# The second layer in blocks of 512 tokens instead of 256, with 512 moving columns in its first product

## The chip, the cores and the metric

One NeuronCore of a Trainium2 chip runs the whole program. The metric is the device time of one execution in microseconds. Names of engines: PE is TensorE, PEld its weight loads, DVE VectorE, ACT ScalarE, POOL GpSimd, SP the engine that issues the DMAs.

## What is computed

```python
attn = attention(q, k, v, phi)        # 8 x 8 x 576 x 64, with a memory of 32
x = attn as (4608 tokens, 512)
h = x @ moe_w_in                      # 512 -> 2048
x = (h - tanh(h)) @ moe_w_out         # 2048 -> 512: first layer
h = x @ moe2_w_in
g = where(h > 0, h, exp(min(h, 0)) - 1)
out = g @ moe2_w_out                  # second layer
```

All inputs are float32. A product is made of three matmuls: each operand is split into a high part (rounded) and the remainder, a = 0 and a = 1 in the code, and high·high, high·low and low·high are added up in PSUM.

## The kernel before, in words

Attention and the first layer come first (`Attention`, `Moe1`), in blocks of 288 tokens and four sweeps over the hidden units. The first layer's output is left in DRAM as four partial sums, `x2_dram`, which the second layer adds up. The second layer (`Moe2`) goes over 18 blocks of `TB` = 256 tokens and in each over 8 slices `pg` of 256 hidden units: 144 steps, called one by one from `step2`. All instructions stand in program order on their engines; nothing is rearranged by a scheduler.

One step of `step2` issues, in this order:

- `h_unit`, the first product: two halves `j` of 128 hidden units, for each 12 matmuls (4 pieces of the contraction, three part products) with the weights as the stationary operand and 256 tokens of `x` as moving columns. Both halves lie in one PSUM tile of 128 x 512.
- `e_a`, `e_b`, `e_c`, the elementwise part of min, tanh, exp and max on DVE and ACT; `e_c`, one step later, splits the result into high (ACT, L469) and low (POOL, L470).
- `prep`, a piece of the next block's input: `load_x` (one of the four partial sums into the pool `xr`, three buffers), `add_x` (DVE, L426), and `split_x` (high on ACT, L432, low on POOL, L433).
- `o_unit`, the second product of two steps earlier (`LAG2`): for each of two groups `tg` of 128 tokens six matmuls with the elementwise result as the stationary operand and 512 output columns. In the last slice of a block each group is copied from PSUM into a tile `o` (L486 on ACT, L488 on DVE; the pool `o` has two buffers) and stored.

The accumulators of `o_unit` are two tags of the PSUM pool `ps_o` with two buffers each; `ps_m` has three banks for the first product, `ps_c` one.

```python
        def step2(idx):
            if idx < len(seq):
                n, pg = seq[idx]
                m2.h_unit(n, pg)
                m2.e_a(n, pg)
            if 1 <= idx <= len(seq):
                m2.e_c(*seq[idx - 1])
            if idx < len(seq):
                m2.e_b(n, pg)
                prep(n + 1, pg)
            if idx >= LAG2:
                m2.o_unit(*seq[idx - LAG2])
```

The hand-over: in the last four blocks of the first layer (`bi` 60 to 63) a queue `soon` prepares the second layer's first block. One entry is taken in each half `i` of such a block before the first `x_unit`, and from `bi` 61 on a second one ahead of the second. That second place stands, on DVE, before the copy of `x` (L397) and the first layer's elementwise instructions of `g_c` (L367 to L369). Steps 0 and 1 of the second layer are issued among the last eight `x_unit`s of the first.

Of the kernel before, what the change touches and what calls it, by code (L numbers as in the profile page):

```python
# [24 lines left out]
NPG = DFF // 256  # L25
NSW = 4
TB = 256
# [379 lines left out]
class Moe2:  # L407


    def __init__(self, tc, x2_dram, out):  # L410
        self.tc, self.nc, self.x2_dram, self.out = tc, tc.nc, x2_dram, out
        self.x, self.h, self.e, self.acc = {}, {}, {}, {}
        self.w = {}

    def load_x(self, n, sw):
        t = self.xr_p.tile([128, 4, TB], F32, tag="xr", name="xr")
        self.nc.sync.dma_start(out=t, in_=self.x2_dram[sw, :, :, n * TB:(n + 1) * TB])
        if sw == 0:
            self.x[n] = [t]
        else:  # L420
            self.x[n].append(t)

    def add_x(self, n):
        raw = self.x[n]
        t = raw.pop(1)
        self.nc.vector.tensor_tensor(raw[0], raw[0], t, op=ALU.add)  # L426

    def split_x(self, n):
        nc = self.nc
        raw = self.x[n][0]  # L430
        x = self.x_p.tile([128, 2, 4, TB], F32R, tag="x", name="x")
        nc.scalar.activation(x[:, 0], raw, ACTF.Copy)  # L432
        nc.gpsimd.tensor_tensor(x[:, 1], raw, r32(x[:, 0]), op=ALU.subtract)  # L433
        self.x[n] = x

    def h_unit(self, n, pg):
# [10 lines left out]
        self.h[n, pg] = [ps]  # L447

    def e_a(self, n, pg):
        nc, w = self.nc, self.h[n, pg]  # L450
        hm = self.ew.tile([128, 2, TB], F32, tag="hm", name="hm")
        t = self.ps_t.tile([128, 2, TB], F32, tag="c", name="t_ps")
# [5 lines left out]
    def e_b(self, n, pg):  # L458
        nc = self.nc
        ps, hm, t = self.h[n, pg]  # L460
# [4 lines left out]
    def e_c(self, n, pg):  # L465
        nc = self.nc
        hm = self.h.pop((n, pg))[1]
        e = self.e_p.tile([128, 2, 2, TB], F32R, tag="e", name="e")
        nc.scalar.activation(e[:, 0], hm, ACTF.Copy)  # L469
        nc.gpsimd.tensor_tensor(e[:, 1], hm, r32(e[:, 0]), op=ALU.subtract)  # L470
        self.e[n, pg] = e

    def o_unit(self, n, pg):
        nc = self.nc
        if pg == 0:
            self.acc[n] = [self.ps_o.tile([128, DM], F32, tag=f"o{i}", name="o_ps") for i in range(2)]
        e, w4 = self.e.pop((n, pg)), self.w["o", pg]
        for tg in range(2):
            for j in range(2):
                for i, (a, b) in enumerate(((0, 0), (0, 1), (1, 0))):  # L480
                    nc.tensor.matmul(self.acc[n][tg], lhsT=e[:, a, j, 128 * tg:128 * tg + 128], rhs=w4[:, b, j, :],  # L481
                                     start=(pg == 0 and j == 0 and i == 0), stop=(pg == NPG - 1 and j == 1 and i == 2))
            if pg == NPG - 1:
                o = self.o_p.tile([128, DM], F32, tag="o", name="o")
                if tg == 0:
# [17 lines left out]
def moe_kernel(tc, q, k, v, phi, w1, w2, w3, w4, out):  # L503
    nc = tc.nc
    with ExitStack() as top, tc.manual_schedule():
# [156 lines left out]
        def open_l2():  # L662
# [6 lines left out]
            m2.x_p = pool("xs", 2)  # L669
# [11 lines left out]
        seq = [(n, pg) for n in range(NB2) for pg in range(NPG)]  # L681
        LAG2 = 2

        def prep(n, step):

            if n < NB2:
                if step in (3, 4, 5):
                    m2.add_x(n)
                if step < NSW:
                    m2.load_x(n, step)  # L690
                if step == 6:
                    m2.split_x(n)

        def step2(idx):
            if idx < len(seq):
                n, pg = seq[idx]
                m2.h_unit(n, pg)
                m2.e_a(n, pg)
            if 1 <= idx <= len(seq):
                m2.e_c(*seq[idx - 1])  # L700
            if idx < len(seq):
                m2.e_b(n, pg)
                prep(n + 1, pg)
# [4 lines left out]
        for bi, (ss, bp, sub, j) in enumerate(blocks):  # L708
            sw, n = 2 * ss + sub, 4 * bp + j
            if bi == 60:  # L710
# [3 lines left out]
                soon = deque([steps(0), steps(1), steps(2), steps(3), weight("i", 0), steps(4, 5), weight("i", 1),  # L714
                              steps(6), weight("o", 0), weight("i", 2), weight("o", 1)])
# [90 lines left out]
        first = deque([("o", 2, w_first), ("i", 3, w_next), ("o", 3, w_next)])  # L806
# [7 lines left out]
        for ctx in (ps_h_ctx, l1c, l1a):  # L814
            ctx.close()
        m2.ps_o = new(l2, "ps_o", 2, space=PSUM)
# [3 lines left out]
                      if (kind, k) not in (("o", 4), ("i", NPG)))  # L820
# [35 lines left out]
```

## Time and profile before

| | |
|---|---|
| median of 3 runs | 1751.77 us (1746.34 to 1754.0) |
| span of the profiled execution | 1749.5 us |
| PE busy, share of the span | 1637.8 us, 94% |
| PEld | 1513.9 us, 87% |
| DVE | 1222.6 us, 70% |
| ACT | 954.2 us, 55% |
| POOL | 760.9 us, 43% |
| DMA | 238.42 MB, mean 136 GB/s |
| mean granted clock of PE | 0.970 |

The span runs from the first to the last instruction of the profiled execution; the device time of a run holds what lies around it too, and the median stands 2.3 us above this span. Matmuls are pipelined and the trace models their ends, so a PE that is busy may still be standing before each matmul; how fast it goes is read from the starts of consecutive units in the chain of waits, not from its busy share.

### The profile page before, as it was taken

The page shows a single profiled execution, that of the slowest core. Times are in us where ns is not written, and L with a number is a line of the kernel's source. Part 1 is how long each engine was busy: PE and PEld are TensorE (multiplying, and loading weights), DVE is VectorE, ACT ScalarE, POOL GpSimd, SP SyncE. Part 2 cuts the span into 40 slices and gives each one's busy share as a digit, 9 for nine tenths or more (in the row PEclk, how much of TensorE's full clock was granted, in tenths as well). Part 3 has the DMA queues.
Part 4 walks back from the last instruction along what each step waited for, and adds up shares of the span by engine and source line. Part 5 has one row for each costly group of instructions (what it writes and reads, how often), then busy time and mean ns, then how long its engine had stood idle before and what let it go on. Part 6 is the DMA issues. An engine that isn't in the chain of part 4 may idle for free.

```text
span 1749.5 us, 30362 instructions
## 1 busy us (share of the span) xinstructions
PE 1637.8 (94%) x11632; PEld 1513.9 (87%) x11632; DVE 1222.6 (70%) x1821; ACT 954.2 (55%) x1713; POOL 760.9 (43%) x537
## 2 busy tenths in 40 slices
PE   5668989988998999999989999999999999999998
PEld 3557878887898999999989999999999999999997
DVE  5769666778899999998965555555555555555554
ACT  2456666677878888888863333333333333333332
POOL 2245545546666667676752222222222222222222
PEclk7669999999999999999999999999999999999999
DMA  8765555467566456666578312211212212111110
GB/s 213 198 177 148 179 158 181 147 199 232 187 211 200 167 182 208 215 223 208 203 230 316 130 60 61 61 54 56 61 61 61 61 61 61 58 52 58 58 31 25
DMA packets 140936, 238.42 MB, mean 136 GB/s; under 512 B 8184, under 2 KB 102392, under 8 KB 138744
## 3 DMA queue, kind: packets, MB, share of 16 engines
q1 hardware_dynamic: 140792, 236.49, 43.3%
q8 instruction: 92, 1.51, 0.4%
q14 instruction: 52, 0.43, 0.1%
HBM read 159.78 MB, written 75.50 MB: 134 GB/s over the span
## 4 chain that ended last, share of the span: by engine, by line
PE 75%; DVE 10%; ACT 5%; DMA 5%; issue 3%; POOL 2%; ACTq 0%; DVEq 0%; POOLq 0%; SPq 0%
PE h_ps L444 23%; PE o_ps L481 23%; PE x_ps L388 15%; PE h_ps L343 8%; PE vw_ps L328 3%; DVE s L368 2%; DMA w_dram<-wst 2%; DVE vw L333 1%; DMA raw<-in_moe_w_in_dram 1%; DMA phi<-in_phi_dram 1%; DVE h_ps L367 1%; DVE s L369 1%; PE km L156 1%; ACT t L354 1%; ACT big L357 1%
## 5 line engine op out<-in xcount | busy, mean ns | idle before, releaser
L388 PE MATMUL x_ps<-g,w 128*128 128x288 f32 x3072 | 442.8, 298 | 13.7 <-ACT x L395 6.7
L470 POOL TENSOR_TENSOR e<-hm,e 128x512 fp32r<-128x512 f32 x144 | 186.5, 1295 | 587.0 <-ACT e L469 442.6
L444 PEld LDWEIGHTS h_ps<-x,wi 128*128 128x128 f32 x3456 | 429.8, 190 | 11.7
L388 PEld LDWEIGHTS x_ps<-g,w 128*128 128x128 f32 x3072 | 421.5, 190 | 18.6 <-ACT x L395 8.0
L444 PE MATMUL h_ps<-x,wi 128*128 128x256 f32 x3456 | 433.2, 282 | 0.0
L481 PE MATMUL o_ps<-wo,e 128*128 128x512 f32 x1728 | 423.8, 394 | 0.7 <-POOL e L470 0.7
L481 PEld LDWEIGHTS o_ps<-wo,e 128*128 128x128 f32 x1728 | 314.9, 188 | 64.9 <-POOL e L470 1.1
L455 ACT ACTIVATE t_ps<-hm 128x512 f32<-128x512 f32 x144 | 86.7, 602 | 514.3 <-DVE hm L454 514.3
L362 POOL TENSOR_TENSOR v<-t,u 128x576 f32<-128x576 f32 x128 | 183.9, 1437 | 197.6 <-ACT u L355 163.9
L343 PE MATMUL h_ps<-p,vw 128*128 128x288 f32 x1536 | 235.8, 304 | 7.9 <-DVE s L369 6.3
L376 POOL TENSOR_TENSOR g<-s,g 128x576 fp32r<-128x576 f32 x128 | 199.0, 1555 | 96.1 <-ACT g L375 91.1
L461 DVE SCALAR_TENSOR_TENSOR hm<-hm,t_ps 128x512 f32<-128x512 f32 x144 | 99.1, 688 | 200.6 <-ACT hm L456 200.6
L343 PEld LDWEIGHTS h_ps<-p,vw 128*128 128x128 f32 x1536 | 217.0, 194 | 12.9 <-issue 7.9
L454 DVE TENSOR_SCALAR hm<-h_ps 128x512 f32<-128x512 f32 x144 | 99.6, 692 | 138.5 <-PE h_ps L444 138.5
L368 DVE SCALAR_TENSOR_TENSOR s<-s,v 128x576 f32<-128x576 f32 x128 | 139.9, 1093 | 3.7 <-POOL v L362 2.6
L354 ACT ACTIVATE t<-h_ps 128x576 f32<-128x576 f32 x128 | 83.2, 650 | 72.7 <-PE h_ps L343 28.4
L369 DVE COPY_PREDICATED s<-big,h_ps 128x576 f32<-128x576 uint32 x128 | 106.6, 833 | 12.0 <-ACT u L355 0.5
L333 DVE TENSOR_TENSOR vw<-vw_ps,vw 64x512 fp32r<-64x512 f32 x128 | 87.8, 686 | 36.5 <-ACT vw L331 34.5
L356 ACT ACTIVATE s<-u,bias 128x576 f32<-128x576 f32 x128 | 99.5, 778 | 24.0 <-POOL g L376 14.6
L328 PE MATMUL vw_ps<-w,vm 128*128 128x256 f32 x480 | 78.9, 304 | 28.2 <-ACT x L395 14.7
L463 DVE TENSOR_TENSOR hm<-hm,h_ps 128x512 f32<-128x512 f32 x144 | 99.0, 687 | 5.0
L462 DVE SCALAR_TENSOR_TENSOR hm<-hm,t_ps 128x512 f32<-128x512 f32 x144 | 98.9, 687 | 4.9
(85 smaller groups left out, 1827.5 us busy)
## 6 DMA issues: line engine op xcount, KB each, us to landing
x_dram<-x SPq DMA_DIRECT2D x128, 288.0 KB
xr<-x_dram SPq DMA_DIRECT2D x72, 512.0 KB
p<-p_dram SPq DMA_DIRECT2D x62, 576.0 KB
raw<-in_moe_w_in_dram SPq DMA_DIRECT2D x32, 512.0 KB
raw<-in_moe_w_out_dram SPq DMA_DIRECT2D x32, 512.0 KB
w_dram<-wst SPq DMA_DIRECT2D x32, 512.0 KB
kv<-in_k_dram SPq DMA_DIRECT2D x16, 576.0 KB
kv<-in_v_dram SPq DMA_DIRECT2D x16, 576.0 KB
```

The costliest lines, as they stand in the source:

```text
L328: nc.tensor.matmul(ps[:, kc], lhsT=vm[:, a, p, :], rhs=wi[:, b, p, :], start=(i == 0), stop=(i == 2))
L333: nc.vector.tensor_tensor(lo, src, r32(hi), op=ALU.subtract)
L343: nc.tensor.matmul(ps[:, j, :NB], lhsT=vw[a][:, kc, 128 * j:128 * j + 128], rhs=p[:, kc, b, :], start=(k == 0), stop=(k == 5))
L354: nc.scalar.activation(t, w[0], ACTF.Tanh)
L362: nc.gpsimd.tensor_tensor(v, t, u, op=ALU.mult)
L368: nc.vector.scalar_tensor_tensor(s, s, G_B, v, op0=ALU.add, op1=ALU.mult)
L369: nc.vector.copy_predicated(s, big.bitcast(U32), d)
L376: nc.gpsimd.tensor_tensor(g[:, 1], s, r32(g[:, 0]), op=ALU.subtract)
L388: nc.tensor.matmul(ps, lhsT=wo[pg][:, a, j, 128 * dm:128 * dm + 128], rhs=g[:, b, j, :], start=(k == 0), stop=(k == 11))
L444: nc.tensor.matmul(ps[:, j], lhsT=w3[:, a, kc, 128 * j:128 * j + 128], rhs=x[:, b, kc, :], start=(k == 0), stop=(k == 11))
L470: nc.gpsimd.tensor_tensor(e[:, 1], hm, r32(e[:, 0]), op=ALU.subtract)
L481: nc.tensor.matmul(self.acc[n][tg], lhsT=e[:, a, j, 128 * tg:128 * tg + 128], rhs=w4[:, b, j, :], start=(pg == 0 and j == 0 and i == 0), s ...
```

## The change

Blocks of 512 tokens: 9 blocks, in each 16 slices `k` of 128 hidden units (`pg, j = divmod(k, 2)` picks the weights), 144 steps as before. `h_unit` has 12 matmuls with 512 moving columns. `o_unit` goes over four groups of 128 tokens with three matmuls each; the four accumulators have one buffer each, so as much PSUM as before. `x` is loaded, added and split in two halves of 256 tokens, four loads each. The first block's two halves are prepared in `soon`, which has 14 entries instead of 11, and some weights are loaded later.

```diff
-TB = 256
+TB = 512
+NU2 = DFF // 128
...
-    def load_x(self, n, sw):
-        t = self.xr_p.tile([128, 4, TB], F32, tag="xr", name="xr")
-        self.nc.sync.dma_start(out=t, in_=self.x2_dram[sw, :, :, n * TB:(n + 1) * TB])
...
+    def load_x(self, n, half, sw):
+        t = self.xr_p.tile([128, 4, TB // 2], F32, tag="xr", name="xr")
+        t0 = n * TB + half * (TB // 2)
+        self.nc.sync.dma_start(out=t, in_=self.x2_dram[sw, :, :, t0:t0 + TB // 2])
+        self.raw.append(t)
...
+    def split_x(self, n, half):
+        nc = self.nc
+        raw = self.raw.pop()
+        if half == 0:
+            self.x[n] = self.x_p[n % 2].tile([128, 2, 4, TB], F32R, tag="x", name="x")
+        hi, lo = (self.x[n][:, t, :, half * (TB // 2):(half + 1) * (TB // 2)] for t in range(2))
...
-        ps = self.ps_h.tile([128, 2, TB], F32, tag="m", name="h2_ps")
-        for j in range(2):
-            k = 0
-            for kc in range(4):
-                for a, b in ((0, 0), (0, 1), (1, 0)):
-                    nc.tensor.matmul(ps[:, j], lhsT=w3[:, a, kc, 128 * j:128 * j + 128], rhs=x[:, b, kc, :],
-                                     start=(k == 0), stop=(k == 11))
-                    k += 1
+        pg, j = divmod(k, 2)
...
+        ps = self.ps_h.tile([128, TB], F32, tag="m", name="h2_ps")
+        i = 0
+        for kc in range(4):
+            for a, b in ((0, 0), (0, 1), (1, 0)):
+                nc.tensor.matmul(ps, lhsT=w3[:, a, kc, 128 * j:128 * j + 128], rhs=x[:, b, kc, :],
+                                 start=(i == 0), stop=(i == 11))
+                i += 1
...
-            self.acc[n] = [self.ps_o.tile([128, DM], F32, tag=f"o{i}", name="o_ps") for i in range(2)]
+            self.acc[n] = [self.ps_o.tile([128, DM], F32, tag=f"o{i}", name="o_ps") for i in range(TB // 128)]
...
+        for tg in range(TB // 128):
+            for i, (a, b) in enumerate(((0, 0), (0, 1), (1, 0))):
+                nc.tensor.matmul(self.acc[n][tg], lhsT=e[:, a, 128 * tg:128 * tg + 128], rhs=w4[:, b, j, :],
+                                 start=(k == 0 and i == 0), stop=(k == NU2 - 1 and i == 2))
+            if k == NU2 - 1:
...
-                if tg == 0:
+                if tg % 2 == 0:
...
         def prep(n, step):
             if n < NB2:
+                half, step = divmod(step, NU2 // 2)
...
-                soon = deque([steps(0), steps(1), steps(2), steps(3), weight("i", 0), steps(4, 5), weight("i", 1),
-                              steps(6), weight("o", 0), weight("i", 2), weight("o", 1)])
+                soon = deque([steps(0), steps(1), steps(2), steps(3), weight("i", 0), steps(4, 5, 6), steps(8),
+                              steps(9), steps(10), weight("o", 0), steps(11), steps(12, 13, 14), weight("i", 1),
+                              weight("o", 1)])
...
-        first = deque([("o", 2, w_first), ("i", 3, w_next), ("o", 3, w_next)])
+        first = deque([("i", 2, w_first), ("o", 2, w_next), ("i", 3, w_next)])
...
-        m2.ps_o = new(l2, "ps_o", 2, space=PSUM)
+        m2.ps_o = new(l2, "ps_o", 1, space=PSUM)
+        m2.x_p.append(new(l2, "xs2", 1))
```

What this moves on the engines shows in three places of the program's order. Square brackets name the engine or DMA queue on which an instruction waits, as far as the program asks for it.

PE where one block's accumulators pass to the next; a row is one or several matmuls, `x9` nine of them. Before, a first product and the next block's first second product:

```order
L444 MATMUL h_ps<-x,wi_11283 128x256 [waits DVE_49,PE_49]
L444 MATMUL h_ps<-x,wi_11283 128x256 x23
L481 MATMUL o_ps<-wo_11264,e 128x512 [waits Activation_49]
L481 MATMUL o_ps<-wo_11264,e 128x512
L481 MATMUL o_ps<-wo_11264,e 128x512 [waits Pool_49]
L481 MATMUL o_ps<-wo_11264,e 128x512 x9
```

With the change, the same place:

```order
L443 MATMUL h_ps<-x,wi_11395 128x512 [waits DVE_49]
L443 MATMUL h_ps<-x,wi_11395 128x512 x11
L480 MATMUL o_ps<-wo_11285,e 128x512 [waits Activation_49]
L480 MATMUL o_ps<-wo_11285,e 128x512
L480 MATMUL o_ps<-wo_11285,e 128x512 [waits Pool_49]
L480 MATMUL o_ps<-wo_11285,e 128x512 [waits DVE_49]
L480 MATMUL o_ps<-wo_11285,e 128x512 x2
L480 MATMUL o_ps<-wo_11285,e 128x512 [waits Activation_49]
L480 MATMUL o_ps<-wo_11285,e 128x512 x2
L480 MATMUL o_ps<-wo_11285,e 128x512 [waits DVE_49]
L480 MATMUL o_ps<-wo_11285,e 128x512 x2
```

The first product has 12 matmuls of 512 columns instead of 24 of 256, and the next block's first second product waits at each of its four accumulators, in turn for ACT and DVE, where before it waited for its own operands alone.

DVE at the same place; `o<-o_ps` is the copy of an accumulator, the row behind it the next step's minimum (L454 before, L453 with the change). Before:

```order
L463 TENSOR_TENSOR hm<-hm,h_ps 128x512 [waits DVE_49]
L488 COPY o<-o_ps 128x512 [waits DMAHW3_49,DMAHW2_49,PE_49]
L454 TENSOR_SCALAR hm<-h_ps 128x512 [waits PE_49,Pool_49]
L461 SCALAR_TENSOR_TENSOR hm<-hm,t_ps 128x512 [waits Activation_49]
L462 SCALAR_TENSOR_TENSOR hm<-hm,t_ps 128x512 [waits DVE_49]
```

With the change:

```order
L462 TENSOR_TENSOR hm<-hm,h_ps 128x512 [waits DVE_49]
L487 COPY o<-o_ps 128x512 [waits DMAHW7_49,DMAHW6_49,PE_49]
L487 COPY o<-o_ps 128x512 [waits DMAHW2_49,DMAHW3_49,DVE_49,PE_49]
L453 TENSOR_SCALAR hm<-h_ps 128x512 [waits PE_49,Pool_49]
L460 SCALAR_TENSOR_TENSOR hm<-hm,t_ps 128x512 [waits Activation_49]
L461 SCALAR_TENSOR_TENSOR hm<-hm,t_ps 128x512 [waits DVE_49]
```

There are two copies ahead of the next minimum instead of one, and the second waits for DMAs that read the buffer of `o` (the third and fourth copies take the buffers of the first and second), beside PE.

DVE in the last blocks of the first layer, from the copy of `x` of one unit on. Before:

```order
L397 COPY x<-x_ps 128x288 [waits DMAHW0_49,PE_49]
L367 TENSOR_TENSOR h_ps<-h_ps,t 128x2x288 [waits Activation_49]
L368 SCALAR_TENSOR_TENSOR s<-s,v 128x576 [waits Activation_49,Pool_49]
L369 COPY_PREDICATED s<-big,h_ps 128x576 [waits DVE_49,Activation_49]
L397 COPY x<-x_ps 128x288 [waits DMAHW2_49,PE_49]
L367 TENSOR_TENSOR h_ps<-h_ps,t 128x2x288 [waits Activation_49]
L368 SCALAR_TENSOR_TENSOR s<-s,v 128x576 [waits Activation_49,Pool_49]
```

With the change (lines moved by one):

```order
L398 COPY x<-x_ps 128x288 [waits DMAHW0_49,PE_49]
L368 TENSOR_TENSOR h_ps<-h_ps,t 128x2x288 [waits Activation_49]
L369 SCALAR_TENSOR_TENSOR s<-s,v 128x576 [waits Activation_49,Pool_49]
L370 COPY_PREDICATED s<-big,h_ps 128x576 [waits DVE_49,Activation_49]
L424 TENSOR_TENSOR xr<-xr 128x1024 [waits DMAHW4_49,DMAHW3_49]
L424 TENSOR_TENSOR xr<-xr 128x1024 [waits DMAHW6_49,DVE_49]
L424 TENSOR_TENSOR xr<-xr 128x1024 [waits DMAHW1_49,DVE_49]
L398 COPY x<-x_ps 128x288 [waits DMAHW2_49,PE_49]
L368 TENSOR_TENSOR h_ps<-h_ps,t 128x2x288 [waits Activation_49]
L369 SCALAR_TENSOR_TENSOR s<-s,v 128x576 [waits Activation_49,Pool_49]
```

Three additions stand between the elementwise work of two units, each with a load to wait for; before, DVE has nothing there.

## Rows read from the trace of the kernel before

**Rows 1.** The page, 40 slices of the span, busy tenths and granted clock in tenths.
```profile
PE   5668989988998999999989999999999999999998
...
PEclk7669999999999999999999999999999999999999
```

**Rows 2.** Chain of waits from 1303 us (start us, us, engine, tile, line, instructions).
```profile
1308.00 2.75 PE o_ps L481 x12
1310.75 2.82 PE h_ps L444 x24
...
1324.74 2.81 PE o_ps L481 x12
...
1333.18 2.88 PE h_ps L444 x24
```

**Rows 3.** Timeline 1251 to 1266 us (start us, us, engine, line, operation, operands; idle before).
```profile
1254.30 0.58 ACT L486 ACTIVATE o<-o_ps 128x512 f32<-128x512 f32 x1
...
1255.95 0.69 DVE L488 COPY o<-o_ps 128x512 f32<-128x512 f32 x1
...
1257.21 2.91 PE L481 MATMUL o_ps<-wo,e 128*128 128x512 f32 x12
1257.49 0.69 DVE L454 TENSOR_SCALAR hm<-h_ps 128x512 f32<-128x512 f32 x1 [0.85 <-PE h_ps L444]
...
1260.19 1.30 POOL L470 TENSOR_TENSOR e<-hm,e 128x512 fp32r<-128x512 f32 x1 [4.38 <-PE o_ps L481]
```

**Rows 4.** Timeline 1300 to 1312 us.
```profile
1300.96 0.68 DVE L488 COPY o<-o_ps 128x512 f32<-128x512 f32 x1
...
1302.51 0.52 SPq L417 DMA_DIRECT2D xr<-x_dram  x1
```

**Rows 5.** DMA in slices of 0.25 us: GB/s 1254 to 1264, tenths 1299 to 1309.
```profile
GB/s 0 0 0 0 0 0 41 262 238 295 180 33 0 0 66 123 213 164 221 188 82 16 8 25 12 102 164 225 344 377 389 381 111 0 0 0 0 0 0 0
...
DMA  0000002727941098951285999982000000000000
```

**Rows 6.** Chain of waits at the end of the kernel.
```profile
1745.01 0.69 DVE o L488
```

**Rows 7.** Timeline 880 to 930 us.
```profile
899.55 4.83 DVE L426 TENSOR_TENSOR xr<-xr 128x1024 f32<-128x1024 f32 x2
...
899.76 3.22 PE L343 MATMUL h_ps<-p,vw 128*128 128x288 f32 x12 [5.93 <-DVE s L369]
...
909.04 1.05 ACT L432 ACTIVATE x<-xr 128x1024 fp32r<-128x1024 f32 x1
...
910.63 2.40 POOL L433 TENSOR_TENSOR x<-xr,x 128x1024 fp32r<-128x1024 f32 x1
...
914.45 1.98 DVE L368 SCALAR_TENSOR_TENSOR s<-s,v 128x576 f32<-128x576 f32 x1 [0.93 <-POOL v L362]
...
917.26 0.44 DVE L397 COPY x<-x_ps 128x288 f32<-128x288 f32 x1
...
922.36 3.03 PE L444 MATMUL h_ps<-x,wi 128*128 128x256 f32 x24
```

**Rows 8.** Chain of waits 878 to 931 us.
```profile
881.94 13.80 DMA xr<-x_dram
...
902.98 4.57 PE x_ps L388 x24
907.55 1.62 PE h_ps L343 x12
...
919.33 3.19 PE x_ps L388 x24
```

**Rows 9.** Line L426 from 880 to 1000 us (ns min/median/max).
```profile
L426 DVE TENSOR_TENSOR xr<-xr x7: 1217/1220/2432, 895.8 to 997.2; 128x1024 f32<-128x1024 f32 x7
```

**Rows 10.** Stretches: window, us, busy us of PE, PEld, DVE, ACT, POOL; clock, DMA, GB/s.
```profile
905.00:905.50 0.50, 0.50 (x4) 0.50 (x4) 0.50 (x2) 0.00 (x0) 0.00 (x0) 0.50 0.84 183
```

**Rows 11.** Stretch of first product, same columns.
```profile
1305.20:1307.70 2.50, 2.50 (x23) 2.50 (x22) 1.44 (x3) 0.00 (x0) 1.29 (x1) 1.00 0.23 82
```

More of the change, by code (lines that the diff above doesn't have):

```diff
@@ L428, in split_x @@
[L428 to L436 removed]
+        self.w, self.raw = {}, []
+    def load_x(self, n, half, sw):
[3 more added lines that the diff above has]
+        self.raw.append(t)
@@ L453, in e_a @@
+        self.h[n, k] = [ps]
+    def e_a(self, n, k):
+        nc, w = self.nc, self.h[n, k]
+        hm = self.ew.tile([128, TB], F32, tag="hm", name="hm")
+        t = self.ps_t.tile([128, TB], F32, tag="c", name="t_ps")
         w += [hm, t]
@@ L463, in e_b, with e_c, o_unit @@
         nc.vector.tensor_tensor(hm, hm, ps, op=ALU.max)
-    def e_c(self, n, pg):
+    def e_c(self, n, k):
         nc = self.nc
-        hm = self.h.pop((n, pg))[1]
-        e = self.e_p.tile([128, 2, 2, TB], F32R, tag="e", name="e")
+        hm = self.h.pop((n, k))[1]
+        e = self.e_p.tile([128, 2, TB], F32R, tag="e", name="e")
         nc.scalar.activation(e[:, 0], hm, ACTF.Copy)
         nc.gpsimd.tensor_tensor(e[:, 1], hm, r32(e[:, 0]), op=ALU.subtract)
-        self.e[n, pg] = e
-    def o_unit(self, n, pg):
+        self.e[n, k] = e
+    def o_unit(self, n, k):
         nc = self.nc
-        if pg == 0:
-            self.acc[n] = [self.ps_o.tile([128, DM], F32, tag=f"o{i}", name="o_ps") for i in range(2)]
[L477 to L483, printed above, removed]
+        pg, j = divmod(k, 2)
+        if k == 0:
+            self.acc[n] = [self.ps_o.tile([128, DM], F32, tag=f"o{i}", name="o_ps") for i in range(TB // 128)]
+        e, w4 = self.e.pop((n, k)), self.w["o", pg]
+        for tg in range(TB // 128):
[3 more added lines that the diff above has]
+            if k == NU2 - 1:
                 o = self.o_p.tile([128, DM], F32, tag="o", name="o")
-                if tg == 0:
+                if tg % 2 == 0:
                     nc.scalar.activation(o, self.acc[n][tg], ACTF.Copy)
@@ L668, in open_l2 @@
             m2.xr_p = pool("xr", 3)
-            m2.x_p = pool("xs", 2)
+            m2.x_p = [pool("xs", 1)]
             m2.ew = pool("ew", 2)
@@ L680, in moe_kernel @@
         NB2 = NT // TB
-        seq = [(n, pg) for n in range(NB2) for pg in range(NPG)]
+        seq = [(n, k) for n in range(NB2) for k in range(NU2)]
         LAG2 = 2
@@ L686, in prep @@
             if n < NB2:
+                half, step = divmod(step, NU2 // 2)
                 if step in (3, 4, 5):
-                    m2.add_x(n)
+                    m2.add_x()
                 if step < NSW:
-                    m2.load_x(n, step)
+                    m2.load_x(n, half, step)
                 if step == 6:
-                    m2.split_x(n)
+                    m2.split_x(n, half)
         def step2(idx):
             if idx < len(seq):
-                n, pg = seq[idx]
-                m2.h_unit(n, pg)
-                m2.e_a(n, pg)
+                n, k = seq[idx]
+                m2.h_unit(n, k)
+                m2.e_a(n, k)
             if 1 <= idx <= len(seq):
@@ L701, in step2 @@
             if idx < len(seq):
-                m2.e_b(n, pg)
-                prep(n + 1, pg)
+                m2.e_b(n, k)
+                prep(n + 1, k)
             if idx >= LAG2:
```

26 lines of the change are left out of this document (9 added, 17 removed).

## The prediction

> **What bounds the kernel now.** I read the page's forty slices first: from slice 22 on TensorE (PE) is at 9 tenths or more, its clock at full [rows 1]. That is the second layer, the only stage that the change touches apart from the hand-over into it, so I read its chain of waits next. Through the eight steps of a 256-token block the chain holds nothing but PE: a unit of the first product (24 matmuls, 2.82 to 2.88 us), then one of the second (12 matmuls, 2.75 to 2.81 us), eight times without a gap (16 such rows) [rows 2]. DVE, ACT and POOL wait for PE there. So in this layer time is won by shorter PE units and lost by anything that makes PE wait; there are 18 × 8 = 144 steps. The execution profiled spans 1749.5 us; the median of the three runs is 1751.8, 2.3 us more, which I carry along as it is.
>
> **The change, part by part.**
>
> *1. 24 matmuls of 256 columns become 12 of 512.* The steps stay 144 (9 blocks × 16 slices), with the same products. Nothing in this trace has a first product at 512 columns; the nearest rows are those of the second product, 12 matmuls of 512 columns each with a weight load of its own. The middle of the units is 2.85 us against 2.78 [rows 2], that is 118.8 ns for 256 columns and 231.7 for 512: most of a matmul's excess over its columns seems to go with the columns, little with the instruction. If a unit of the first product takes what one of the second does, a step gains 0.07 us: 144 × 0.07 = **−10.1 us**. Bounds from the same rows: slowest first against fastest second unit, 2.88 − 2.75 = 0.13, −18.7 us; fastest against slowest, 2.82 − 2.81 = 0.01, −1.4 us. A loss isn't excluded by a mechanism, but no unit of 512 columns took longer than one of 2 × 256. I take the middle.
>
> The Trainium skill ("TensorE: Matmul & The Clock Gate", section "Back-to-back issue gap") has columns ÷ 2.4 GHz plus about 2.5 ns for each warm matmul: 109.2 ns at 256 columns, 215.8 at 512. The rows are 9.6 and 15.9 ns above that, so they disagree. By the rule, 1728 matmuls fewer give an estimated −4.3 us, and the sum below would end at +6.5 instead of +0.7.
>
> *2. Four single accumulators.* Before, a block's two accumulators have two buffers each; now the next block's first second-product unit writes where the last one has just been read out. Four copies go through the pool `o`, which still has two buffers: the third and fourth copy wait until the stores of the first and second have landed. In the trace ACT copies accumulator 0 at 1254.30 and DVE accumulator 1 at 1255.95 to 1256.64; the next second-product unit starts at 1257.21 [rows 3]. With three matmuls for each accumulator it would reach the fourth after nine, 9 × 0.232 = 2.09 us, at 1259.30. The store of accumulator 1 has landed about 2.1 us after its copy in one place (copy's end 1301.64, data until about 1303.75) and 2.6 to 3.4 in another (data until 1259.25, a remnant of 8 to 25 GB/s to 1260.0) [rows 4, 5]. With 2.5 the fourth copy runs from 1259.2 to 1259.9, and PE waits about 0.6 us; with 2.1, 0.25; with 3.4, 1.55. Accumulator 2 is no problem: its copy on ACT can start near 1257.0 and is wanted at 1258.6. Behind the waiting fourth copy on DVE stands the next slice's minimum (before at 1257.49 [rows 3]), 2.4 us late; with it ACT's tanh and exp and POOL's subtraction (1260.19, 1.30 long) come 2.4 late, ending at 1263.9. Their reader, the third matmul of the next second-product unit, was due two units (5.6) and two matmuls (0.46) after 1257.21, and is itself 0.6 late: 1263.9. So that chain costs next to nothing more. Eight boundaries: 8 × 0.6 = **+5 us** (2 to 12).
>
> *3. The tail.* After the last unit the same four copies run with no cover. Before, the last copy ran from 1745.01 to 1745.70 right behind the last unit [rows 6], which so began about 1745.0 − 2.78 = 1742.2; accumulator 1 is complete after six matmuls and copied by 1744.3, its store lands 2.1 to 2.6 later, and accumulator 3 is copied by 1747.1 to 1747.6: **+1.8 us** (1.4 to 2.7).
>
> *4. The first block needs twice the tokens.* Eight loads of `xr` instead of four, six DVE additions, two splits, before step 0, and they are put into the last blocks of the first layer. Up to the fifth entry of the queue everything is as before, the stop of 5.9 us included in which DVE waits for the second `xr` load (issued 881.94, landed after 13.80) and PE stands until 899.76 [rows 7, 8]. The first half's split now comes early and hides; POOL's 2.40 us at 910.63 fall away, behind which `v` and so DVE's L368 waited [rows 7]. But three additions are then queued on DVE between the gating work of two units, before `x` is copied; the last one waits for a load that can be issued only when the first of the three has freed its buffer. In the trace DVE reaches that place at 917.26; without POOL's split up to 2.2 us sooner, say 916.2. An addition takes 1.22 us, or 2.43 in the crowded stretch [rows 9]. At the shorter: addition to 917.4, load issued 917.5, landed 3.4 later as the undisturbed one (issued 1302.51 [rows 4], data until about 1305.9 [rows 5]), 920.9; addition 1.2, split 1.05 on ACT, 2.40 on POOL [rows 7], some 0.3 of hand-offs: 925.8. PE's first unit of the second layer started at 922.36 [rows 7] and needs POOL's half with its second matmul. That is 3.4 late at the shorter and 5.8 with both additions at the longer; I take **+4 us** (2.4 to 7, by that and by where DVE is). The clock was granted at half for a while after the 5.9 us stop, which made 36 matmuls take 7.79 us where the same take 4.81, 3.0 us more [rows 7, 8, 10]; the stop forecast is shorter, and I put no such loss into the sum.
>
> *5. At nothing:* the elementwise work (144 × the same 128x512 shapes; DVE waited 0.85 us even at a boundary [rows 3]), the 72 stores and 72 loads, and the weights, each now wanted at half the pace. If those come late, PE waits at units 2 to 8 of the first block show it.
>
> Sum: −10.1 + 5 + 1.8 + 4 = **+0.7 us**, so 1750.2 in the span; for the median, 1751.8 and 0.7, I say 1752. No measurable change is what I forecast; about 0.5% (8.8 us) is what a measurement of this kernel can tell from none.
>
> **The rivals.**
>
> *Faster: weight loads set the pace at 256 columns.* In a stretch of first product the weight loads are busy all of the time, 2.50 of 2.50 us [rows 11]. Were they what the 256-column units wait for, half of them gone would bring the unit to the fastest second unit, 2.75: −18.7. With stores landing in 2.1 us: −18.7 + 2 + 1.8 + 2.4 = −12.5, 1739 us. Against it: those bars overlap one another, and 12 matmuls of 288 columns took 1.62 us [rows 8], 135 ns each, 16 ns more than at 256 where 32 more columns alone would be 13 at the full clock; a weight-load pace would be blind to them. The Trainium skill ("Perfetto Trace Analysis", section "Identifying the Most-Contended Engine") judges PE by the weight loads' busy share rather than the matmuls'; by that rule this rival holds, and the 288-column rows speak against it.
>
> *Slower: the first block comes late.* One place, the three additions, and one price: the stop. If both additions go at 2.43 and DVE comes late, PE stops for 7 us, longer than the 5.9 us after which the clock was at half, and with the 3.0 that this cost there the part is 10 instead of 4: 1758. If the last load also lands as the slow one did (13.80 instead of 3.4 [rows 8]), the stop is 3.4 + 10.4, and −10.1 + 5 + 1.8 + 13.8 + 3.0 = +13.5, 1765 us. From a landing of some 9 us on it decides the sign. For it: the weights go through the same queue there. Against: when that load is issued only one of them and small stores lie ahead of it.
>
> *No gain in the columns.* The excess goes with the columns altogether, or the weights' and the block's places in memory give 2.81 us: −1.4 + 5 + 1.8 + 4 = +9.4, 1761 us. For it: 118.8 ns doubled is 237.5, near the slowest second unit's 234. Against: no row reaches it.
>
> **How the numbers follow.** The forecast 0.50 (1744 to 1760); weight-load pace 0.20; late first block 0.18, of which 0.14 beyond 0.5%; no gain in the columns 0.12. So faster 0.20, same 0.54, slower 0.26. The range takes the forecast's own, most of the fast rival (1739) and the slow ones up to just under the worst landing's 1765: 1738 to 1764.
>
> **What would show it.** Right: first-product units of 12 in 2.75 to 2.81 us in the chain; at eight boundaries 0.2 to 1.6 us of PE waiting for a DVE copy of `o_ps`, and DVE waiting for the store of `o`; a PE stop of 2.4 to 7 us at the first second-layer unit, released by POOL's split; the kernel's last copy starting some 3 us after the one before it on DVE. Wrong: first-product units clearly under 2.75 or over 2.81; boundaries without a wait, or with several us; a stop at the hand-over under 2 or over 7 us, or a half clock behind it.

## The result, and the profile after

| | median (lowest to highest), 6 runs each |
|---|---|
| before | 1747.40 us (1745.85 to 1754.00) |
| with the change | 1762.29 us (1760.00 to 1767.73) |
| ratio | 1.0074, 95% interval 1.0053 to 1.0096 |

The change makes the kernel 0.74% slower, about 13 us by the ratio: more than the 0.5% that the prediction took a measurement to tell from nothing. The execution profiled spans 1760.4 us (its own time 1762.18).

The page of the changed kernel: busy tenths and granted clock in forty slices, and the two products of the second layer (line, engine, operation, operands, count | busy us, mean ns | idle before, its releaser).

```profile
PE   5568989988998999999979999999999999999998
...
PEclk9669999999999999999998999999999999999999
...
L443 PE MATMUL h_ps<-x,wi 128*128 128x512 f32 x1728 | 426.2, 395 | 9.0 <-ACT x L432 7.0
L480 PE MATMUL o_ps<-wo,e 128*128 128x512 f32 x1728 | 426.6, 394 | 7.3 <-DVE o L487 6.6
```

The layer still belongs to PE, as in [rows 1]. New are the 7 of the 21st slice (8 before) with the 8 of the clock behind it, which is the hand-over, and two idle times that name their causes: PE waited for ACT's split of `x`, and for DVE's copies of `o`.

The chain of waits over one block boundary (start us, us, engine, tile, line, instructions):

```profile
1308.44 0.69 DVE o L487
...
1309.15 0.52 SPq L498
...
1309.71 2.44 DMA out_dram<-o
...
1312.27 0.70 DVE o L487
...
1313.02 0.98 PE o_ps L480 x3
1313.99 2.76 PE h_ps L443 x12
1316.75 2.75 PE o_ps L480 x12
1319.50 2.72 PE h_ps L443 x12
```

Beside [rows 2], the first product has come down from 2.82 to 2.88 us to 2.72 to 2.82, where the second is. Over all 141 units of the steady part its mean is 2.846 us before and 2.778 now, that of the second product 2.779 and 2.781. But once in a block the chain leaves PE: copy, issue of the store on SP, the store itself, copy, PE. The same place in the timeline:

```profile
1306.78 0.58 ACT L485 ACTIVATE o<-o_ps 128x512 f32<-128x512 f32 x1
...
1308.44 0.68 DVE L487 COPY o<-o_ps 128x512 f32<-128x512 f32 x1
...
1309.60 2.20 PE L480 MATMUL o_ps<-wo,e 128*128 128x512 f32 x9
1309.85 0.60 ACT L485 ACTIVATE o<-o_ps 128x512 f32<-128x512 f32 x1 [2.49 <-PE h_ps L443]
1312.27 0.69 DVE L487 COPY o<-o_ps 128x512 f32<-128x512 f32 x1 [3.15 <-DMA out_dram<-o]
...
1313.01 0.53 PEld L480 LDWEIGHTS o_ps<-wo,e 128*128 128x128 f32 x3 [1.63 <-DVE o L487]
```

PE does nine of its twelve matmuls and stands before the fourth accumulator. This happens eight times; from the start of such a unit to the start of the next one it takes 3.53 to 4.27 us instead of 2.78. The list of waits counts them (engine and line, what it waited for: us in all, times, longest):

```profile
DVE o L487 <- DMA out_dram<-o: 26.0, 9, 3.2
...
DVE xr L424 <- DMA xr<-x_dram: 15.7, 4, 7.4
...
PEld o_ps L480 <- DVE o L487: 10.1, 8, 1.6
```

Its second line is the hand-over: DVE waits four times for `xr`, 15.7 us, where before it was once, 7.9. The longest, 7.4, is the stop that was there before as well. The chain behind it:

```profile
900.55 14.70 DMA xr<-x_dram
...
915.35 1.88 DVE xr L424
...
917.24 6.00 DMA xr<-x_dram
...
923.33 1.24 DVE xr L424
...
924.59 1.06 ACT x L432
...
925.72 2.76 POOL x L433
...
928.53 5.06 PE h_ps L443 x11
```

And the stretches around it (window, us, busy us and count of PE, PEld, DVE, ACT, POOL, then granted clock, DMA share, GB/s):

```profile
920.00:923.00 3.00, 0.00 (x0) 0.00 (x0) 0.00 (x0) 0.00 (x0) 0.00 (x0) 1.00 1.05 389
923.00:925.00 2.00, 0.00 (x0) 0.00 (x0) 1.67 (x3) 0.41 (x1) 0.00 (x0) 0.70 1.05 440
925.00:930.00 5.00, 2.27 (x5) 1.48 (x6) 3.20 (x6) 4.14 (x7) 4.28 (x3) 0.50 0.76 288
```

For three microseconds no engine computes at all while the DMA engines are full. PE stands for 6.95 us, does one matmul, stands for another 2.04, and then runs 11 matmuls in 5.06 us at half clock, where they take 11 × 0.2315 = 2.55 at full. Over the whole hand-over PE stands for 15.4 us where it stood for 6.3, and is busy for 58.6 where it was for 56.3.

So the time went like this in the two profiled executions, before to after:

| part | us |
|---|---|
| 141 first products, 2.846 to 2.778 | −9.5 |
| eight boundaries, mean excess 1.15 | +9.2 |
| tail: start of the last 36 second-product matmuls to the end, 14.22 to 16.89 | +2.7 |
| hand-over: issue of the first `xr` load to the first second-product unit, 62.6 to 74.0 | +11.4 |
| sum | +13.8 |

The second products make up the remaining 0.3 of 14.1. The two spans are only 10.9 us apart, since the part ahead of the first `xr` load, which the change doesn't touch, was 3.2 us shorter in the second execution (876.38 against 879.57).

### The profile page after: what moved, and what is told of

Read it like the earlier page. It is cut to its first block, busy times and chain, and to the rows that moved or that the text cites. A ratio compares the mean times of both kernels' runs of the same rounds, so it can differ in the third digit from the quotient of the medians.

```text
span 1760.4 us, 26781 instructions
## 1 busy us (share of the span) xinstructions
PE 1631.5 (93%) x9904; PEld 1425.9 (81%) x9904; DVE 1224.9 (70%) x1821; ACT 955.3 (54%) x1713; POOL 759.3 (43%) x537
## 4 chain that ended last, share of the span: by engine, by line
PE 72%; DVE 10%; ACT 7%; DMA 5%; issue 3%; POOL 2%; SPq 0%; DVEq 0%; ACTq 0%; POOLq 0%
PE h_ps L443 22%; PE o_ps L480 20%; PE x_ps L389 16%; PE h_ps L344 9%; PE vw_ps L329 3%; DMA xr<-x_dram 2%; DMA out_dram<-o 1%; ACT t L355 1%; DVE s L369 1%; ACT big L358 1%; DVE s L370 1%; ACT u L356 1%; DMA kv<-in_v_dram 1%; DMA phi<-in_phi_dram 1%; DVE vw L334 1%
## 5 line engine op out<-in xcount | busy, mean ns | idle before, releaser
L443 PE MATMUL h_ps<-x,wi 128*128 128x512 f32 x1728 | 426.2, 395 | 9.0 <-ACT x L432 7.0
L443 PEld LDWEIGHTS h_ps<-x,wi 128*128 128x128 f32 x1728 | 326.0, 189 | 85.3 <-ACT x L432 7.2
L480 PEld LDWEIGHTS o_ps<-wo,e 128*128 128x128 f32 x1728 | 323.1, 188 | 87.9 <-DVE o L487 10.1
L454 ACT ACTIVATE t_ps<-hm 128x512 f32<-128x512 f32 x144 | 86.7, 602 | 493.3 <-DVE hm L453 493.3
L453 DVE TENSOR_SCALAR hm<-h_ps 128x512 f32<-128x512 f32 x144 | 99.5, 691 | 121.9 <-PE h_ps L443 120.6
L357 ACT ACTIVATE s<-u,bias 128x576 f32<-128x576 f32 x128 | 99.5, 778 | 23.5 <-POOL g L377 14.1
```

The lines of the kernel that those rows point to most:

```text
L443: nc.tensor.matmul(ps, lhsT=w3[:, a, kc, 128 * j:128 * j + 128], rhs=x[:, b, kc, :], start=(i == 0), stop=(i == 11))
L480: nc.tensor.matmul(self.acc[n][tg], lhsT=e[:, a, 128 * tg:128 * tg + 128], rhs=w4[:, b, j, :], start=(k == 0 and i == 0), stop=(k == NU2 - ...
```

## The experiments

Two stretches are compared in every run: the hand-over (issue of the first `xr` load to the first second-product unit) and the rest of the layer (from there to the end). The theory: boundaries and tail cost what they cost because `o` has two buffers; the hand-over because its last loads land late and PE stops. The rivals: single accumulators make PE wait whatever `o` has; the gain in the columns is one of place, not of columns; the additions' place on DVE, not the loads, makes the hand-over late.

| run | hand-over | rest | ratio to before (95%) |
|---|---|---|---|
| before | 62.6 | 807.3 | |
| the change | 74.0 | 810.1 | 1.0074 (1.0053 to 1.0096) |
| e1_o4 | 75.3 | 798.6 | 1.0023 (1.0008 to 1.0039) |
| e2_cols256 | 73.4 | 820.7 | 1.0158 (1.0136 to 1.0181) |
| e3_xfirst | 68.8 | 810.0 | 1.0058 (1.0036 to 1.0080) |
| e4_early | 69.1 | 798.8 | 0.9979 (0.9960 to 0.9998) |
| e5_late | 66.8 | 799.8 | 0.9990 (0.9971 to 1.0008) |
| e6_both | 65.9 | 799.8 | 0.9976 (0.9961 to 0.9990) |
| e7_before_late | 64.0 | 808.2 | 1.0001 (0.9988 to 1.0013) |
| e8_order | 63.0 | 799.8 | 0.9954 (0.9938 to 0.9970) |

The stretches are those of one profiled execution each. Each ratio is against runs of the kernel before from the same round (e1 to e4, e5 to e7, e8), and the intervals reach 0.1 to 0.2% to either side, 2 to 4 us: two versions closer than that are not told apart by their ratios.

**Four buffers for `o`.** The changed kernel with

```diff
-        m2.o_p = new(l2, "o", 2)
+        m2.o_p = new(l2, "o", 4)
```

> The changed kernel with four buffers in the pool o instead of two. My theory: the eight waits at block boundaries (0.7 to 1.5 us each in the changed kernel's chain, 9.2 us in all) and 2.6 us of the tail come from the copies of accumulators 2 and 3, which wait until the stores of 0 and 1 have landed; so all eight vanish, the tail shrinks, and the time falls by 11 to 12 us against the changed kernel, to about 3 us above the kernel before. Rival: the single accumulators themselves are the cause (the copy comes too late behind the elementwise work on DVE); then PE still waits at each boundary for a DVE copy, 0.5 us or more, with no store behind it, and at most half of the 12 us comes back.

The rest falls by 11.5 us, as expected; the hand-over is 1.3 us longer in this execution, and by the ratios the whole gains 9 us. A boundary in its timeline:

```profile
1306.55 1.07 ACT L485 ACTIVATE o<-o_ps 128x512 f32<-128x512 f32 x2
...
1308.20 1.28 DVE L487 COPY o<-o_ps 128x512 f32<-128x512 f32 x2
...
1309.37 2.88 PE L480 MATMUL o_ps<-wo,e 128*128 128x512 f32 x12
```

Each pair of copies runs back to back, all twelve matmuls go through, and no second-product unit takes over 3 us. So the boundaries are the buffers' alone; single accumulators cost PE nothing. Of the tail 1.0 us stays (15.20 against 14.22), and it lies behind the copies: the last one comes 5.44 us after the last 22 matmuls begin, as before, but eight store issues in a row instead of four then hold SP.

**256 columns again.** The changed kernel with each first-product unit as two halves of 256 tokens, 24 matmuls, everything else in place:

```diff
+        for half in (slice(0, 256), slice(256, 512)):
...
+                    nc.tensor.matmul(ps[:, half], lhsT=w3[:, a, kc, 128 * j:128 * j + 128], rhs=x[:, b, kc, half],
+                                     start=(i == 0), stop=(i == 11))
```

> The changed kernel with each first-product unit as two groups of 12 matmuls with 256 moving columns, all else as changed. My theory: the columns are worth 0.067 us a unit (2.85 against 2.78), so 144 units cost 9.5 us more than the changed kernel, about 24 us above the kernel before, and the chain shows first-product units of 2.82 to 2.88 us again. Rival: the shorter units of the changed kernel come from where weights and x lie in memory, not from the columns; then units stay at 2.72 to 2.81 and the time does not move by more than 2 us against the changed kernel.

Its chain of waits in the steady part:

```profile
1319.62 2.87 PE h_ps L445 x24
1322.49 2.75 PE o_ps L482 x12
```

The mean goes back to 2.857 us with the new places in memory and the new order of weights, and the rest grows by 10.7 (141 × 0.078 = 11.0). So the gain goes with the columns and not with the places in memory. Twice the columns are also half the matmuls and half the weight loads; which of these it is, no run tells apart. By the ratios the run lost 15 us against the changed kernel, some 5 more than the two stretches. The part ahead of the first `xr` load is 1.3 us longer (877.70 against 876.38); the rest is not explained and no more than the two intervals allow.

**Weights behind the loads.** The changed kernel with the first two weights taken from between the `xr` loads; the last two entries of `soon` now issue two weights each:

```diff
-                soon = deque([steps(0), steps(1), steps(2), steps(3), weight("i", 0), steps(4, 5, 6), steps(8),
-                              steps(9), steps(10), weight("o", 0), steps(11), steps(12, 13, 14), weight("i", 1),
-                              weight("o", 1)])
+                soon = deque([steps(0), steps(1), steps(2), steps(3), lambda: None, steps(4, 5, 6), steps(8),
+                              steps(9), steps(10), lambda: None, steps(11), steps(12, 13, 14),
+                              lambda: [weight("i", 0)(), weight("o", 0)()],
+                              lambda: [weight("i", 1)(), weight("o", 1)()]])
```

> The changed kernel with the first weights of the second layer issued behind the last load of xr, additions and loads at the same places as changed. My theory: the hand-over's 12 us come from loads of xr that land late because 1 MB weight loads lie ahead of them in the DMA queues (14.7 and 6.0 us after issue in the changed kernel); with the weights behind, they land in some 4 to 8 us, the stop of PE of 9 us shrinks to 3 to 5 and the half clock behind it goes, 5 to 8 us less than the changed kernel, unless the weights now come late themselves, which would show as PE waiting for wi. Rival: the three additions between two units on DVE are the cause, whatever the loads do; then the time falls by less than 2 us.

DVE at the three additions, and the chain behind them:

```profile
913.14 4.16 DVE L424 TENSOR_TENSOR xr<-xr 128x1024 f32<-128x1024 f32 x2
...
919.33 1.23 DVE L424 TENSOR_TENSOR xr<-xr 128x1024 f32<-128x1024 f32 x1 [2.02 <-DMA xr<-x_dram]
```

```profile
914.95 4.28 DMA xr<-x_dram
...
924.53 5.06 PE h_ps L443 x11
```

In the changed kernel DVE waited 3.42, 1.40 and 3.49 us at these additions; now it waits 2.02 us at the third alone. The trace records sixteen completion signals for each load. By the last of them the load that the first addition needs landed after 9.67 us instead of 14.70, the one before it after 10.62 instead of 15.65, and the last one after 4.28 instead of 6.00, with additions and loads at the same places of the program. So weights ahead of a load in the DMA queue make it some 2 to 5 us later. They are not all of it: the load issued at 895.09 landed after 3.78, and what still lies ahead of the two slow ones is a `p` of the first layer, issued at 895.70, beside stores of `x`. Twelve of their sixteen signals are in 5.7 us after issue and the last four only at 9.67 and 10.62. `p` itself gives one signal early (896.67) and four at its end (906.51 to 907.92), as if it ran on four of the sixteen DMA engines and the loads queued behind it there; no run moves a `p` to test that.

The hand-over wins 5.2 us, the low end of what was expected, and by the ratios the whole wins 3. PE now stops twice, with starts 2.83 and 1.40 us apart around one matmul, and the half clock comes all the same (0.50 from 924 to 930), with its 5.06 us for 11 matmuls. That this would go with the long stop was wrong.

**Loads early, additions two half-blocks later.** The changed kernel with five `xr` buffers, three for `o`, and the tokens' halves kept apart so that loads can run ahead:

```diff
+                soon = deque([load(0, 0, 1), load(0, 2, 3), load(1, 0), weight("i", 0), add(0, 2), load(1, 1, 2),
+                              add(0, 1, True), load(1, 3), weight("o", 0), weight("i", 1), add(1, 1), add(1, 1),
+                              add(1, 1, True), weight("o", 1)])
...
+        m2.o_p = new(l2, "o", 3)
```

> The changed kernel with three buffers in o and another hand-over: five buffers of xr, all loads issued as early as buffers allow and each addition some two half-blocks (10 us and more) behind its load. My theory: boundaries and tail as with four buffers of o (11 to 12 us less), and neither the late stop (9 us and the clock) nor the earlier one of 6 us that the kernel before has too; the columns' 9.5 us are then a gain: 10 to 18 us faster than the kernel before, about 1730 to 1738 us. If the additions' place on DVE were the cause of the hand-over's loss, it would stay at 5 us or more and the time near the kernel before's less 3 us.

Missed: 0.21% faster than before, 3.7 us, where 10 to 18 was expected. Its chain says part of why:

```profile
877.31 15.22 DMA xr<-x_dram
...
893.88 15.13 DMA xr<-x_dram
...
919.04 2.75 POOL x L434
...
921.84 5.06 PE h_ps L444 x11
```

From start to start, the first stop shrinks to 2.44 us from 5.55, but a weight and a `p` are issued from 887.97 on, ahead of the next loads; those take 15 us again, and PE stops at new places (3.08, 2.34 and 2.82 us). Other transfers are waited for now:

```profile
890.74 1.86 PE L344 MATMUL h_ps<-p,vw 128*128 128x288 f32 x12 [2.15 <-DMA p<-p_dram]
...
906.24 0.46 DVE L398 COPY x<-x_ps 128x288 f32<-128x288 f32 x1 [4.83 <-DMA x_dram<-x]
```

At the additions DVE stands only once, 3.35 us. Starting the loads earlier took away one wait, and others came in its place; how far the loads themselves make `p` and the stores late is not told apart.

**Last additions behind the first layer's elementwise work.** The changed kernel with four buffers for `o`, the last additions and split at other places, and steps 0 and 1 later:

```diff
-                              steps(9), steps(10), weight("o", 0), steps(11), steps(12, 13, 14), weight("i", 1),
+                              steps(9), steps(10), weight("o", 0), steps(11), lambda: None, weight("i", 1),
...
-            if len(xq) in (7, 4):
-                step2(0 if len(xq) == 7 else 1)
+            if len(xq) in (7, 5):
+                steps(*((12, 13) if len(xq) == 7 else (14,)))()
+            if len(xq) == 2:
+                step2(0)
...
+        step2(1)
```

> The changed kernel with four buffers in o (as e1_o4), its last three additions and the second split moved behind the first layer's last elementwise work, and the second layer's steps 0 and 1 moved behind six and all of the first layer's last seven x units instead of ahead of seven and four of them. Nothing is computed less or loaded earlier. My theory: the hand-over's remaining loss (in e1_o4 PE stands 6.8 and 2.8 us before the first unit, and its first unit takes 2.5 us more at the half clock) is PE standing at a unit whose input comes late, with 11 us of other matmuls queued behind it; with these ahead of it the stop goes to under 2 us and the half clock with it: 9 to 12 us less than e1_o4, some 1740 us, 7 to 10 under the kernel before. Rival: the hand-over is bound by the DMA queues or by the elementwise work of the first layer's last units, which then stop PE just as long at another place; then less than 4 us is gained on e1_o4.

Half met: 8.5 us of hand-over less than with four buffers alone, and by the ratios some 6 us in all. Of the stop at the first unit 2.13 us is left (from start to start), and no half clock follows it (1.00 from 934 to 946). But one addition stayed in its place, and its load, issued at 906.33, took 14.57 us. So the loads land as late as in the changed kernel and most of the loss goes even so: it takes both, late loads and work that stands behind what waits for them, on DVE behind the additions and on PE behind the first unit. e5 moves both, so these two are not told apart. A control puts the steps at the same later places in the kernel before:

```diff
-            if len(xq) in (7, 4):
-                step2(0 if len(xq) == 7 else 1)
+            if len(xq) == 2:
+                step2(0)
...
+        step2(1)
```

> Control: the kernel before with the second layer's steps 0 and 1 in e5_late's later places, all else as before. Before, PE does not stand at the first unit, so my theory gives no change, within 3 us. If it became faster by 5 us or more, e5_late's gain would come from the place of the steps as such and not from a stop that the change made.

No change, as expected: in the kernel before, the later place of the steps neither wins nor costs. Both edits in one, e4's early loads with its five `xr` and three `o` buffers and e5's late places; against e4:

```diff
-                              add(0, 1, True), load(1, 3), weight("o", 0), weight("i", 1), add(1, 1), add(1, 1),
-                              add(1, 1, True), weight("o", 1)])
+                              add(0, 1, True), load(1, 3), weight("o", 0), weight("i", 1), add(1, 1), lambda: None,
+                              lambda: None, weight("o", 1)])
...
+            if len(xq) in (7, 5):
+                add(1, 2 if len(xq) == 7 else 0, len(xq) == 5)()
+            if len(xq) == 2:
+                step2(0)
...
+        step2(1)
```

> e5_late's late steps and additions with e4_early's five buffers of xr and early loads (three buffers in o). My theory: beside e5_late's gain the first stop, 6 us in the kernel before and 2.4 in e4_early, falls by some 3 to 4 us, if the loads that come earlier do not stop something else: 1736 to 1740 us. Rival: the DMA queues bound the stretch, as e4_early's new short stops suggest; then it is no faster than e5_late by more than 1 us.

Missed as well: 0.24% faster than before, 4.2 us, where 1736 to 1740 us was expected. PE's gaps are all short now (3.37, 1.70, 1.21 and 2.13 from start to start), yet the hand-over is 65.9, 3.3 us over that of before. The first of them does not wait for an addition but for `p`:

```profile
894.43 3.22 PE L344 MATMUL h_ps<-p,vw 128*128 128x288 f32 x12 [3.08 <-DMA p<-p_dram]
```

These 12 matmuls take 3.22 us, at half clock; the same take 1.77 at full.

**Order as well as place.** e6 with all weights behind all eight loads, the first two additions one place later, and all three additions of the second half behind the first layer's elementwise work:

```diff
-                soon = deque([load(0, 0, 1), load(0, 2, 3), load(1, 0), weight("i", 0), add(0, 2), load(1, 1, 2),
-                              add(0, 1, True), load(1, 3), weight("o", 0), weight("i", 1), add(1, 1), lambda: None,
-                              lambda: None, weight("o", 1)])
+                soon = deque([load(0, 0, 1), load(0, 2, 3), load(1, 0), idle, idle, add(0, 2),
+                              load(1, 1, 2), add(0, 1, True), load(1, 3), weight("i", 0), idle, weight("o", 0),
+                              idle, idle])
...
-        first = deque([("i", 2, w_first), ("o", 2, w_next), ("i", 3, w_next)])
+        first = deque([("i", 1, w_first), ("o", 1, w_first), ("i", 2, w_first), ("o", 2, w_next), ("i", 3, w_next)])
...
-                add(1, 2 if len(xq) == 7 else 0, len(xq) == 5)()
+                add(1, 3 if len(xq) == 7 else 0, len(xq) == 5)()
```

> e6_both with the second layer's weights issued behind all eight loads of xr instead of among them, the first two additions one place later, and the second half's three additions all behind the first layer's last elementwise work. If the loads of xr in the hand-over are held up by what lies ahead of them in the DMA queues (as e3_xfirst's 14.7 to 5.5 us says), the stops left in e6_both (3.4 at the first addition, 1.7 and 1.2 some 15 us later, 2.1 with the half clock at the first unit) shrink by some 3 to 5 us together: about 6 to 9 us under the kernel before, 1742 us. If the queues' volume (the eight loads, the stores and the loads of p, whatever their order) is the bound, it moves by less than 2 us against e6_both, which was 0.24% under the kernel before.

Met in the time: 0.46% faster than before (8 us by the ratio, interval 5 to 11), the lowest ratio of all, though its interval and e6's overlap. Its timeline:

```profile
898.20 1.23 DVE L425 TENSOR_TENSOR xr<-xr 128x1024 f32<-128x1024 f32 x1 [2.27 <-DMA xr<-x_dram]
...
906.36 0.99 SPq L419 DMA_DIRECT2D xr<-x_dram  x1
907.41 2.52 SPq L677 DMA_DIRECT2D wi<-w_dram  x1
...
922.56 4.84 DVE L425 TENSOR_TENSOR xr<-xr 128x1024 f32<-128x1024 f32 x3
```

The last `xr` load is issued at 906.36 and only then the first weight; the three additions run as one piece without a wait; DVE's only wait for `xr` is 2.27 us. The hand-over is 63.0, near the 62.6 of before the change.

The way was another than expected, though. The two loads with the longest way landed hardly sooner, after 13.60 and 14.08 us, against 15.09 and 15.21 in e6, and PE's stops did not shrink. Here is the whole hand-over, with six microseconds inside it, in e6:

```profile
877.08:943.02 65.94, 58.79 (x372) 55.12 (x371) 39.56 (x44) 32.82 (x58) 28.18 (x19) 0.92 0.89 283
...
894.00:900.00 6.00, 5.57 (x23) 5.60 (x24) 3.59 (x5) 1.22 (x3) 0.04 (x1) 0.50 0.98 330
```

and in e8:

```profile
880.89:943.88 62.99, 55.93 (x372) 52.39 (x370) 39.97 (x44) 33.63 (x59) 28.34 (x19) 0.97 0.85 286
...
894.00:900.00 6.00, 5.03 (x38) 4.83 (x37) 3.73 (x5) 1.77 (x4) 2.27 (x2) 1.00 0.80 261
```

PE stands 65.94 − 58.79 = 7.15 us in e6 and 62.99 − 55.93 = 7.06 in e8. The 2.9 us between the two are busy time for the same count of matmuls: in e6 the clock is at half behind the first stop, where PE waits 3.08 us for `p`; in e8 the wait for `p` there is 0.97 and the clock stays full. So in these two executions the step from e6 to e8 is a stretch of half clock that does not come. What each of the three edits has of it is not told apart.

It is also the version in which most of the columns' gain reaches the end. In the traces −9.5 of columns, +1.2 of tail, +1.0 of the first second-product unit (3.76 us) and −0.2 of the others make −7.5 in the rest, and with +0.4 of hand-over −7.1.

## Why the prediction was right or wrong

1762 us lies in the range, but beyond the 0.5% and on the side that I gave 0.26; the likeliest case, no measurable change, did not come. That it lies in the range is in part luck: the +13.8 of the traces on the 1751.8 that I started from would be 1765.6, outside it. Step by step:

1. **Columns: right.** −10.1 forecast, −9.5 measured; first-product units at 2.72 to 2.82 in the chain, as named. The rival of the weight loads, as priced (2.75 throughout, −18.7), falls with the mean of 2.778, that of no gain (2.81) too, and e2 shows that the gain is not one of places in memory. By the formula in the Trainium skill ("TensorE: Matmul & The Clock Gate", section "Back-to-back issue gap"), which the page gives for a single matmul in isolation and not for a stream with weight loads, the 1728 matmuls saved would have been worth an estimated 4.3 us, 2.5 ns each. My use of it for a stream was beyond what the page says. The steady part won 9.5 with 1692 of them, 5.6 ns each, and a matmul of 512 columns takes 231.5 ns and not 215.8; the measurement decides.
2. **Boundaries: the mechanism right, the size off by half.** 8 × 0.6 = 5 forecast, 8 × 1.15 = 9.2 measured, inside the 2 to 12. The mis-sized term is the landing of the store: I took 2.5 us from the end of the copy, read off the data in the DMA slices [rows 5]. In the chain shown it is 3.14: 0.52 to issue the store's first piece on SP, 2.44 from the issue of the second to its landing, and hand-offs of 0.18. Over the eight boundaries DVE stands 2.51 to 3.23 us for it, 2.88 in the mean. That is 0.4 of the 0.55 us that each boundary cost more than forecast; the remaining 0.15 is not broken down.
3. **Tail: the mechanism right, +1.8 forecast, +2.7 measured**, the upper bound. Of the 2.7, 2.3 lie ahead of the last copy and 0.4 behind it; the stores of the first two groups are issued in pieces one behind the other on SP, as the chain at the end has it:

```profile
1752.68 0.38 SPq L498
...
1753.10 2.32 DMA out_dram<-o
...
1755.54 0.69 DVE o L487
```

The last copy starts 3.67 us after the one before it on DVE (1751.87).

4. **Hand-over: the step that failed.** +4 forecast (2.4 to 7), +11.4 measured. Put on the clock of the first `xr` load (876.38 here, 879.57 before, so 3.2 is added), each link can be laid beside the forecast. The first of the three additions starts at 918.5 instead of 916.2, since its own load, of which I had asked nothing, landed after 14.70 us (+2.3). It takes 1.88 and its buffer's load is issued 0.6 later than that spacing allowed (+0.6). That last load lands after 6.00 instead of 3.4 (+2.6). From there to POOL's end it is 5.24 instead of 4.9 (+0.3). Together 5.8 on the 3.4 that I had worked out, so PE is 9.2 late, and the half clock costs 2.5 more: 11.7. The failing sentence is "landed 3.4 later as the undisturbed one": I priced a load in the most crowded stretch by a load in an empty one, although [rows 8] shows 13.80 for one in the same queue some 35 us earlier. The step's other fault was to put the half clock at nothing because the stop forecast was shorter than the 5.9 us seen; in e3 it came after starts 2.83 and 1.40 us apart.

Why they land so late: e3 shows the weights' part, 5.0 of the 14.70 and 1.7 of the 6.00; what `p` has of the rest is not shown.

So of the cases written down, "the first block comes late" is what happened. Its mildest form put 10 us there, half clock included, which is near the 11.4; its sum was +6.7 against the +13.8 of the traces, and 4.2 of what is missing are the boundaries. The absolute time hides some of the miss: the kernel before has a median of 1747.4 over the six runs, 4.4 less than the 1751.8 that I started from.

## What to carry to other kernels

A buffer count that was enough for two outputs per block must be looked at again when there are four: the wait is a store's whole way, issue on the queue included, and is read off the chain, not off the transfer's data. A load is priced by the transfers that share its queue and its stretch of time. Where it gates the next stage, nothing that is needed later goes ahead of it in the queue, and the transfers behind it, here `p`, are looked at as well. An instruction that waits for it stands behind the work that does not need it. When a stop shrinks or stays, the clock behind it is to be looked at before the gain is put down to the stop. A steady gain of 0.07 us per unit is worth having only if the seams (hand-over, boundaries, tail) are laid out for the new block size as well; with that done, in e8, the same change is 0.46% faster instead of 0.74% slower.

## What the runs showed of the hardware

- A matmul's excess over its columns at full clock grew with the columns: 118.6 ns for 256 and 231.5 for 512 (unit means of 2.846 / 24 and 2.778 / 12), so 5.7 ns saved for each pair made one, where the excess over 2.4 columns per ns is 11.9 and 18.2. Why it grows was not tried.
- The clock fell to half after stops that were short and broken by one matmul: starts 2.83 and 1.40 us apart in e3, 2.34 and 2.82 in e4. The same stop, 2.13 us before the second matmul of the first unit, was followed by a mean clock of 0.66 from 931 to 936 in e6 and of 1.00 from 934 to 946 in e5. What decides is not shown.
- A load of the same 512 KB landed in 3.73 to 4.03 us where little else was in flight (the fourth load of the kernel before, the change, e1, e2, e3, e5 and e7), in 9.67 and 10.62 behind a `p` (e3), and in 14.70 and 15.65 behind a `p` and a weight of 1 MB (the change). Of the sixteen completion signals the twelfth came after 3.6, 5.7 and 9.9 us in one load of each kind (the fourth of the change, the sixth of e3, the sixth of the change): behind a `p` the last four are late, behind a weight as well all of them.
- The DMA engines can be full at very different rates: 250 GB/s at a share of 1.05 from 905 to 910 in the changed kernel, 389 at the same share from 920 to 923. What makes the same engines move so much less was not tried.
